# The order of the last weight loads in a decode kernel, and the queue that loads x

## The chip, the core and the metric

The kernel runs on one NeuronCore of a Trainium2 chip. The metric is the device time of one execution in microseconds (us), as the median of several runs. All inputs lie in HBM (the chip's main memory) as bfloat16, and the kernel moves them into SBUF (on-chip memory of 128 partitions) with DMA transfers that run on 16 DMA engines.

## The reference

One token per batch entry goes through an attention block with a sliding window over a key and value cache, and then through a gated MLP block. Batch B = 8, model width D = 512, 32 query heads, 8 key/value heads, head size 128, window W = 2048 of 8192 cached positions.

```python
def _A_ref(x, k_cache, v_cache, wq, wo):
    q = (x @ wq).reshape(B, 1, 32, 128).transpose(0, 2, 1, 3)
    k = repeat(k_cache[:, :, Sk - W:, :], 4, axis=1)
    v = repeat(v_cache[:, :, Sk - W:, :], 4, axis=1)
    p = softmax(einsum("bhqd,bhkd->bhqk", q, k) * 128 ** -0.5)
    o = einsum("bhqk,bhkd->bhqd", p, v)
    return o.transpose(0, 2, 1, 3).reshape(B, 1, 4096) @ wo

def _B_ref(x, w1, w2, w3, w4):
    # with one token every shifted branch is zero, so hs = 0 and x1 = x
    return x + gelu(layernorm(x) @ w3) @ w4

h   = x + _A_ref(layernorm(x), k_cache, v_cache, wq, wo)
out = h + _B_ref(layernorm(h), w1, w2, w3, w4)
```

The loads are: wq 4 MB, the windows of K and of V 32 MB each, wo 4 MB, w3 and w4 1.8 MB each. w1 and w2 are not needed, since the shifted branches vanish for one token.

## The kernel before, in words

The kernel is written engine by engine. Each engine (TensorE, ScalarE, VectorE, GpSimd, SyncE) gets its own list of instructions in a fixed order, and they meet only at semaphores. SyncE (SP) issues nearly all loads, in the order of the list `order`.

**Tiles and slots.** The K window of one batch entry and four heads is one tile of 2 MB, and so is the V window, so there are 16 K tiles (k0 to k15) and 16 V tiles (v0 to v15), two of each for a batch entry. A tile takes one of NS = 10 slots of the buffer `slots`, 16 KB in each of the 128 partitions. The n-th entry of `order` goes into slot n % 10. `free_slot(n)` makes SP wait until entry n - 10 is used up: for a K tile until TensorE has transposed it (`sem_Thi`), for a V tile until its product with the probabilities is done (`sem_PV`). The last two slots hold wq at first, and are free once the queries lie in `qstrip`.

**Order before.** SP first loads wq. Then come k0, k1, and for each batch entry two K tiles and two V tiles by turns. The end of the list is k15, v13, the first half of wo, v14, v15, the rest of wo, w3, w4. The last V tile v15 is loaded in two halves with semaphores of their own (`V_CUT`), wo in four pieces of 16, 8, 4 and 4 heads (`WO_CUT`), and w4 in two pieces of 8 and 6 chunks (`W4_CUT`). Behind v15 SP loads x a second time, into `xr_sb`. The first load of x, into `x_sb`, is issued by ScalarE in `act_warm`.

**The end of the kernel.** `act_exp`, `dve_pT` and `pe_PV` handle the last batch entry (b = 7) once its scores are complete. `pe_PV` multiplies each V tile in 64 matmuls. `dve_combine` writes the attention output into `oT_all`. `pe_proj` then adds x (4 matmuls with an identity) and the output projection, 4 matmuls for each of 32 heads, and waits before heads 0, 16, 24 and 28 for the piece of wo that it needs. `dve_h`, `pe_stats`, `dve_norms` and `act_std_h` form the layer norm of the sum. `pe_h3` waits for w3 and runs 56 matmuls, `act_gelu` follows, and `pe_fin` runs 28 matmuls over the 14 chunks of w4, with a wait at each entry of `W4_CUT`. The result is copied by VectorE and ScalarE and stored by SP.

**Start.** x is needed by `dve_pro1` (its layer norm) and by `pe_zinit`. wq is needed by `pe_q`, whose result VectorE writes into `qstrip`. The first eight K and V tiles need neither, since their slots are free from the start.

## Time and profile before

| What | Value |
|---|---|
| median of 4 runs | 198.11 us (197.84 to 198.3) |
| the profiled execution's own time | 198.49 us |
| its span, first to last instruction | 196.7 us |
| granted TensorE clock, mean | 0.894 |
| busy: TensorE matmul / weight load | 159.8 us / 119.4 us |
| busy: VectorE / ScalarE / GpSimd | 82.6 us / 90.5 us / 4.8 us |
| DMA queue 1 (all of SP's loads) | 10544 packets, 79.19 MB, 96.4% of 16 engines' span |
| DMA queue 8, kind "instruction" | 22 packets, 0.36 MB |

The profile is of one execution. It lies 0.38 us above the median of the four runs, and its own time is 1.8 us longer than its span, which begins with the first and ends with the last of the program's instructions. L409 means line 409 of the kernel file. PE is TensorE's matmul, PEld its weight load, DVE is VectorE, ACT is ScalarE, SPq is a DMA issue by SyncE. "Idle before" is the time that the engine stood idle before an instruction, with what ended it; "issue" there means that no semaphore that the profile shows ended it.

### The profile page before, as it was taken

Reading aid. Unit: us, or ns where it says so; the run is one execution under the profiler, and the core shown is the slowest. Engines: PE = TensorE matmul, PEld = TensorE weight load, DVE = VectorE, ACT = ScalarE, POOL = GpSimd, SP = SyncE. Lnnn points to the kernel's source line nnn. Section 1 sums busy time; section 2 is a strip of 40 time slices with the busy share of each in tenths; the row PEclk is TensorE's granted clock in tenths of the full one; section 3 lists DMA queues with packets and bytes.
Section 4 is the critical chain, followed back from the end, with each engine's and each line's share of the span. In section 5 each row is a group of like instructions: output and inputs, shape, how many; then the busy total and the mean of one; then the engine's idle time right before and its main releaser. Section 6 shows DMA issues by size and latency. Waiting matters only on the chain.

```text
span 196.7 us, 6328 instructions
## 1 busy us (share of the span) xinstructions
PE 159.8 (81%) x2808; PEld 119.4 (61%) x2808; DVE 82.6 (42%) x184; ACT 90.5 (46%) x109; POOL 4.8 (2%) x15
## 2 busy tenths in 40 slices
PE   2037999699989998959997989698989989385465
PEld 0037866486767766647775666576767767185452
DVE  7501445444662375425623653256236614330040
ACT  3301665936573465625643665247436534330040
POOL 8000000000000000000000000000000000000000
PEclk9999999999996999996999999969996969955555
DMA  6999999999999999999999999999999999999980
GB/s 228 433 420 427 443 423 430 430 427 427 428 427 430 432 423 433 423 430 427 430 427 430 427 433 430 422 437 423 433 427 423 427 390 390 425 402 314 407 337 14
DMA packets 10585, 79.58 MB, mean 405 GB/s; under 512 B 680, under 2 KB 4800, under 8 KB 6208
## 3 DMA queue, kind: packets, MB, share of 16 engines
q1 hardware_dynamic: 10544, 79.19, 96.4%
q8 instruction: 22, 0.36, 0.7%
q14 instruction: 3, 0.02, 0.0%
q10 hardware_dynamic: 16, 0.01, 0.0%
HBM read 79.18 MB, written 0.01 MB: 403 GB/s over the span
## 4 chain that ended last, share of the span: by engine, by line
DMA 56%; PE 28%; SPq 9%; issue 3%; DVE 2%; ACT 2%; ACTq 0%
DMA slots<-in_A_k_cache_dram 51%; PE kT_ps L409 16%; PE S_ps L441 6%; DMA slots<-in_A_wo_dram 5%; SPq L268 5%; SPq L262 3%; PE misc L533 3%; PE b L697 2%; DVE pT_sb L507 1%; ACT kT_sb L420 1%; PE misc L667 1%; ACT P_sb L475 1%; SPq L259 1%; PE S_ps L607 0%; PE S_ps L625 0%
## 5 line engine op out<-in xcount | busy, mean ns | idle before, releaser
L420 ACT ACTIVATE kT_sb<-kT_ps 128x1024 bf16<-128x1024 bf16 x64 | 65.6, 1025 | 75.4 <-PE kT_ps L409 75.4
L409 PEld LDWEIGHTS kT_ps<-ident_b,slots 128*128 128x128 bf16 x1024 | 65.1, 106 | 29.8 <-issue 21.4
L409 PE MATMUL kT_ps<-ident_b,slots 128*128 128x128 bf16 x1024 | 74.6, 234 | 7.7 <-DMA slots<-in_A_k_cache_dram 7.7
L426 DVE COPY kT_sb<-kT_ps 128x1024 bf16<-128x1024 bf16 x64 | 43.6, 688 | 61.9 <-PE kT_ps L409 61.9
L441 PE MATMUL S_ps<-kT_sb,qstrip 128*32 128x512 bf16 x256 | 38.4, 613 | 0.0
L533 PEld LDWEIGHTS misc<-pT_sb,slots 128*128 128x128 bf16 x1024 | 27.2, 97 | 7.8 <-issue 6.0
L533 PE MATMUL misc<-pT_sb,slots 128*128 128x16 bf16 x1024 | 28.6, 170 | 3.8 <-DVE pT_sb L507 1.9
L475 ACT ACTIVATE P_sb<-S_ps,mtile 128x1024 bf16<-128x1024 f32 x16 | 17.8, 1115 | 4.7 <-DVE mtile L464 4.4
L409 PE MATMUL kT_ps<-ident_b,P_sb 128*128 128x128 bf16 x128 | 10.0, 226 | 6.6 <-ACT P_sb L475 5.5
L409 PEld LDWEIGHTS kT_ps<-ident_b,P_sb 128*128 128x128 bf16 x128 | 7.5, 100 | 11.7 <-issue 4.9
L507 DVE TENSOR_TENSOR pT_sb<-kT_ps,maskT 128x1024 bf16<-128x1024 bf16 x16 | 10.4, 684 | 0.2
L441 PEld LDWEIGHTS S_ps<-kT_sb,qstrip 128*32 128x32 bf16 x256 | 5.9, 94 | 6.0 <-issue 0.6
L540 DVE TENSOR_TENSOR oT_all<-misc,rL 128x32 bf16<-128x32 f32 x8 | 2.4, 300 | 16.1 <-PE misc L533 16.1
L588 ACT ACTIVATE std<-var,eps_t 128x8 f32<-128x8 f32 x1 | 0.3, 301 | 14.4 <-DVE var L640 14.4
L453 DVE TENSOR_REDUCE mtile<-S_ps 128x1 f32<-128x512 f32 x8 | 5.5, 692 | 3.0 <-PE S_ps L441 3.0
L364 PE MATMUL S_ps<-xlnT,slots 128*128 128x8 bf16 x128 | 3.6, 168 | 3.2 <-DMA slots<-in_A_wq_dram 3.2
L607 PE MATMUL S_ps<-oT_all,slots 128*128 128x8 bf16 x128 | 3.9, 168 | 2.2 <-issue 1.6
L364 PEld LDWEIGHTS S_ps<-xlnT,slots 128*128 128x128 bf16 x128 | 3.5, 104 | 3.3 <-issue 3.3
L344 PE MATMUL b<-ident_b,xln_b 8*128 8x8 bf16 x4 | 0.3, 174 | 6.2 <-DVE xln_b L321 6.2
L607 PEld LDWEIGHTS S_ps<-oT_all,slots 128*128 128x128 bf16 x128 | 3.7, 104 | 2.3 <-issue 1.7
L297 DVE TENSOR_SCALAR ident_f<-iota_f 128x128 f32<-128x128 f32 x1 | 3.9, 3928 | 1.5 <-POOL iota_f L202 1.5
L344 PEld LDWEIGHTS b<-ident_b,xln_b 8*128 8x128 bf16 x4 | 0.2, 114 | 7.1 <-DVE xln_b L321 7.1
(75 smaller groups left out, 57.5 us busy)
## 6 DMA issues: line engine op xcount, KB each, us to landing
slots<-in_A_k_cache_dram SPq DMA_DIRECT2D x16, 2048.0 KB, 41.7
slots<-in_A_v_cache_dram SPq DMA_DIRECT2D x15, 2048.0 KB, 44.3
slots<-in_A_wq_dram SPq DMA_DIRECT2D x1, 4096.0 KB, 12.3
slots<-in_A_wo_dram SPq DMA_DIRECT2D x1, 2048.0 KB, 44.4
slots<-in_A_v_cache_dram SPq DMA_DIRECT2D x2, 1024.0 KB, 13.7
slots<-in_B_w_dram SPq DMA_DIRECT2D x1, 1792.0 KB, 12.0
slots<-in_A_wo_dram SPq DMA_DIRECT2D x1, 1024.0 KB, 16.2
slots<-in_A_wo_dram SPq DMA_DIRECT2D x2, 512.0 KB, 13.4
```

What stands on the lines that cost most here:

```text
L262: e.dma_start(dst, src).then_inc(sem_slot[slot], 16)
L268: e.dma_start(dst[:, f0:f0 + (h1 - h0) * D].rearrange("p (h n) -> p h n", n=D), A_wo[h0 * 128:h1 * 128, :].rearrange("(h p) n -> p h n", p ...
L364: ins = e.matmul(S_ps[:, 0, h * B:(h + 1) * B], wq_v[:, kc, h * DH:(h + 1) * DH], xlnT[:, kc * B:(kc + 1) * B], start=(kc == 0), stop=(kc ...
L409: ins = e.matmul(kT_ps[n % 2][:, c * 128:(c + 1) * 128], src[:, c * 128:(c + 1) * 128], ident_b[:, :], is_transpose=True)
L420: e.activation(kT_sb[:, i % NKT, 0:W // 2], kT_ps[step_of[("k", i)] % 2][:, 0:W // 2], ACT.Copy).then_inc(sem_Elo, 1)
L426: e.tensor_copy(kT_sb[:, i % NKT, W // 2:W], kT_ps[step_of[("k", i)] % 2][:, W // 2:W]).then_inc(sem_Ehi, 1)
L441: ins = e.matmul(S_ps[32 * gl:32 * (gl + 1), b % 2, :], qstrip[:, b, GL * gq + gl, o:o + 32], kv[:, gl, :, :], start=(gq == 0 and qi == 0) ...
L453: ins = e.tensor_reduce(mtile[:, 2, 0:1], S_ps[:, j, :], AX.X, ALU.max)
L475: e.activation(P_sb[:, half * W // 2:(half + 1) * W // 2].rearrange("r (k g) -> r k g", g=GL), s_rep, ACT.Exp, bias=mtile[:, j, 0:1], scal ...
L507: e.tensor_tensor(pT_sb[:, half * hc:(half + 1) * hc, :], kT_ps[n % 2][:, half * W // 2:(half + 1) * W // 2].rearrange("p (c x) -> p c x", ...
L533: ins = e.matmul(ot, slots[:, slot, c * DH:(c + 1) * DH], pt[:, cc, :, o:o + R], start=(n == 0), stop=(n == C - 1), skip_group_check=True)
L607: ins = e.matmul(hT_ps[:, k * B:(k + 1) * B], wo_at(h)[:, k * 128:(k + 1) * 128], oT_all[:, h, :], start=False, stop=(h == H - 1), skip_gr ...
```

## The change

x becomes the first load on SP, ahead of wq, and ScalarE issues no load any more. The second load of x is dropped: `pe_proj` reads `x_sb`, and has no wait for x. At the end of `order` the first half of wo moves behind v14 and v15, so that all of wo follows the last V tile, and w3 and w4 follow as before. w4 is cut into three pieces of 8, 4 and 2 chunks in place of two of 8 and 6. By the slot rule v14 now waits for k11, v15 for v9 and the first half of wo for k12, where before the first half of wo waited for k11, v14 for v9 and v15 for k12. What stands behind them waits for the same entries as before. No compute instruction is added or removed, and their order on each engine is unchanged.

```diff
-        xr_sb = sb([B, D], dt.bfloat16, "xr_sb")
...
-        sem_w4 = [S(f"sem_w4_{i}") for i in range(2)]
+        sem_w4 = [S(f"sem_w4_{i}") for i in range(3)]
...
-        W4_CUT = [0, 8, 14]
+        W4_CUT = [0, 8, 12, 14]
...
-        order += [("wo", 0), ("v", NTILE - 2), ("v", NTILE - 1), ("wo", 1), ("w3", 0), ("w4", 0)]
+        order += [("v", NTILE - 2), ("v", NTILE - 1), ("wo", 0), ("wo", 1), ("w3", 0), ("w4", 0)]
...
         def sp_prog(e):
+            e.dma_start(x_sb[:], A_x.rearrange("b s d -> (b s) d")).then_inc(sem_x, 16)
             e.dma_start(wq_sb, A_wq.rearrange("(p k) n -> p (k n)", k=KC)).then_inc(sem_wq, 16)
...
-                        e.dma_start(xr_sb[:], A_x.rearrange("b s d -> (b s) d")).then_inc(sem_xr, 16)
...
         def act_warm(e):
-            e.dma_start(x_sb[:], A_x.rearrange("b s d -> (b s) d")).then_inc(sem_x, 16)
             e.wait_ge(sem_pool, POOL_EPS)
...
         def pe_proj(e):
...
-            e.wait_ge(sem_xr, 16)
             for k in range(KC):
-                e.matmul(hT_ps[:, k * B:(k + 1) * B], xr_sb[:, k * 128:(k + 1) * 128], ident_b[0:B, 0:B],
+                e.matmul(hT_ps[:, k * B:(k + 1) * B], x_sb[:, k * 128:(k + 1) * 128], ident_b[0:B, 0:B],
                          start=(k == 0), stop=False, skip_group_check=True)
```

## The prediction

> **What bounds the kernel now.** I read the page's slices first.

> ```profile
> PEclk9999999999996999996999999969996969955555
> DMA  6999999999999999999999999999999999999980
> ```

> The DMA engines are full from the second of 40 slices to the 38th. TensorE is busy too (81%), but its waits at the start of a K tile end with that tile's load (7.7 us in 6 waits by the waits view), so the stream of loads sets the pace, and whatever delays its start delays the kernel. The clock stays at half speed in the last five slices.

> The start, from the timeline:

> ```profile
> 0.73 0.40 SPq L236 DMA_DIRECT2D slots<-in_A_wq_dram  x1
> 0.74 0.59 ACTq L287 DMA_DIRECT2D x_sb<-in_A_x_dram  x1
> 1.19 1.91 SPq L262 DMA_DIRECT2D slots<-in_A_k_cache_dram  x3
> ```

> The two issues run side by side. The first wq packet starts at 1.76, and by half-microsecond windows the engines are full from 2.5 on.

> SP's own timeline near the end:

> ```profile
> 124.04 0.38 SPq L268 DMA_DIRECT2D slots<-in_A_wo_dram  x1
> 126.28 36.59 SPq L262 DMA_DIRECT2D slots<-in_A_v_cache_dram  x1
> 162.92 1.33 SPq L259 DMA_DIRECT2D slots<-in_A_v_cache_dram  x2
> 164.30 0.54 SPq L260 DMA_DIRECT2D xr_sb<-in_A_x_dram  x1
> 164.88 11.54 SPq L268 DMA_DIRECT2D slots<-in_A_wo_dram  x3
> 176.46 2.02 SPq L272 DMA_DIRECT2D slots<-in_B_w_dram  x1
> 178.52 2.55 SPq L278 DMA_DIRECT2D slots<-in_B_w_dram  x2
> ```

> An issue behind a large wo piece is held: v14's for 36.59 us, the second wo piece of the later half for 9.04 of the 11.54. Loads still land in order, by their semaphores' updates: k15 158.2, v13 163.1, wo's first half 168.4, v14 173.3, v15's halves 175.8 and 178.3, the wo pieces 181.0, 182.5 and 184.1, w3 188.4, w4's pieces 191.0 and 192.9.

> The end, TensorE's timeline:

> ```profile
> 173.79 3.04 PE L533 MATMUL misc<-pT_sb,slots 128*128 128x16 bf16 x96
> 178.33 0.97 PE L533 MATMUL misc<-pT_sb,slots 128*128 128x16 bf16 x30 [1.49 <-DMA slots<-in_A_v_cache_dram]
> 179.63 0.22 PE L533 MATMUL misc<-pT_sb,slots 128*128 128x16 bf16 x2 [0.33 <-issue]
> ...
> 184.13 0.40 PE L607 MATMUL S_ps<-oT_all,slots 128*128 128x8 bf16 x9 [0.52 <-DMA slots<-in_A_wo_dram]
> 186.18 0.33 PE L607 MATMUL S_ps<-oT_all,slots 128*128 128x8 bf16 x7 [1.64 <-issue]
> ...
> 189.31 1.63 PE L667 MATMUL misc<-uT,slots 128*128 128x8 bf16 x56 [1.61 <-DVE uT L644]
> ...
> 191.30 3.16 PE L697 MATMUL b<-slots,gT 128*8 128x256 bf16 x28
> ```

> Two idle times bear the name "issue": 0.33 before the last two V matmuls and 1.64 inside the last wo piece, though that piece landed at 184.1. Exactly 127 matmuls, with their weight loads about 255 instructions, lie between the two places. Queue 8 carries 22 instruction packets of 16 KB; two of them run from 177.32 to 178.29 and from 183.97 to 184.93. So TensorE runs out of instructions, and goes on 1.2 us after such a packet ends. [...]

> **x ahead of wq on SP.** The nearest row for the price is the same 8 KB load on the same queue, L260: 0.54 us, and 0.04 between issues. The ACT row says 0.59. That puts wq at 1.31 in place of 0.73 and shifts the whole stream by up to 0.65. The lower bound: the first wq packet came 1.03 after its issue, the store's first packet at the end 0.80 after its own (194.96 to 195.76). If that 0.23 is a cost of first use that x now pays, 0.34 remains. Below nothing I exclude, as the wq issue cannot come sooner. I take 0.50. No slack absorbs it, since the engines are full from 2.5 to 178. x itself is hidden: its layer norm waits for VectorE's masks until 6.46. The nine K and V issues behind wq end by 6.4 and become 0.5 later, with wq's packets covering them until 12. ScalarE loses 0.59 of issue time that nothing waits for.

> **The second load of x goes.** 8 packets of some 0.05 us on eight engines, 0.54 us of SP time under full queues, a wait that was long met: -0.05 at most.

> **The order at the end.** The bytes ahead of each wo piece but the first, of w3 and of w4 are the same, so those landings only move by the start's shift. v14 and v15 land one wo half earlier (168.0, then 170.5 and 173.0), and wo's first half at 178.3 in their place, each plus 0.5. Their slots are free in time: k11 and v9 released SP at 124.04 and 126.28, and k12's transposes end at 134.4, forty microseconds ahead of the data. SP's hold behind wo's first half comes later, until about 172.6 (when, as at 162.88 before, about half of its 2048 rows have been moved), and w3's issue becomes some 1 us later than the 176.46 to 178.48 of before. Only w3, w4 and the store stand behind on SP; w3 is needed by the slowest engine at 184.1. Price nothing, under that cover of 4 us; without it, the last rival.

> On TensorE the 1.49 us wait for v15 goes: k15 and the softmax chain still release the V matmuls at 173.79 + 0.5, and 128 at 31.7 ns (3.04 us for 96) would end at 177.85 + 0.5. What is late next is the instruction block, at 179.63 + 0.5 if its packet is as slow as before, then the next at 186.18 + 0.5. So the layer norm, L667 and the start of L697 follow 0.5 later. [...]

> [...]

> **w4 in three pieces.** One more issue, 1.2 us of SP (L278) while its queue is full, and one more wait on TensorE that holds the last four matmuls and the output copy behind it. L697's 28 matmuls ran without a gap before (28 x 105 ns from 191.30), so a smaller last piece has nothing to win unless L697 starts sooner: 0.

> **Sum.** 0.50 - 0.05 - 0 - 0 = +0.45. On the profiled execution that is 198.49 + 0.45 = 198.94, which lies 0.38 above its median; on the median 198.11 + 0.45 = 198.56, say 198.55. A measurement here tells 0.2%, 0.4 us, from no change.

> **Rivals.** [...]

> *Clock regained: faster.* Without the 1.49 us hole TensorE works from 172.6 to 178.3 nearly without a break. The clock's records show it coming back after whole stretches of 3.41 us of K work (158.48 to 161.89). At full clock L697 shrinks from 2.95 to some 1.8 (16 transposes take 1.00 against 1.69), and the end is w4's last piece, 192.9 + 0.5, plus four matmuls and the drain: 193.95 against 194.48, so 197.6. It decides only if V matmuls of 16 columns count as work and the clock then survives the waits for wo. Against: a stretch with 1.7 us of them and a 0.65 gap lost the clock at 158.48, and 5 us of end work did not bring it back.

> [...]

> *Starved by wo.* 4 MB in 1 KB rows now stand in one piece. If wo's next issue is held as long behind the first half as it was before (9.04 us), it comes free at 181.6, while the slowest engine is through at 178.3: with 1 us to the first packet 4.3 us are lost, 202.4, and a hold of half the excess 200.5. It decides once the hold ends after 178. Against: the hold before ended when V's rows ahead were drained, and none stand between now.

> **How the numbers follow.** Forecast +0.35 to +0.65: 0.55. Looser tail: 0.20. Clock regained: 0.14. Starved: 0.11. Slower by over 0.2% is most of the forecast (those over 0.4 us) and the starved case, 0.47 + 0.11 = 0.58; within is the looser tail and the forecast's low end, 0.28; faster 0.14. The range 197.5 to 199.6 takes in the first three and the mild starved cases.

> **What would show it.** Right: L235 (wq) issued near 1.3, k0 landing near 18.4 for 17.9, the last landing near 193.4, no DMA wait at v15's matmuls but "issue" there, and again inside the last wo piece. Wrong: wq's first packet near 1.8 all the same; a granted clock over 0.5 after 175; a wait for wo beyond 178.8; landings of w3 that move by more than the start's shift.

## The result, and the profile after

The changed kernel is slightly slower. Its median is 198.93 us over 54 runs, against 198.36 us over 78 runs of the kernel before, and the ratio is 1.0027 with a 95% interval of 1.0018 to 1.0036. That is +0.53 us on 198.36, where the sum of the prediction gave +0.45 on its own base. The profiled executions of two experiments below (e1 and e4) were slow ones, with spans of 235.2 and 287.9 us, so only their first microseconds are read, and their times come from the other runs.

The start, from the timeline of the kernel after:

```profile
0.73 1.28 ACT L286 ACT_TABLE_LOAD   x1 [0.73 <-PEq L744]
0.73 0.37 SPq L234 DMA_DIRECT2D x_sb<-in_A_x_dram  x1
1.16 0.37 SPq L235 DMA_DIRECT2D slots<-in_A_wq_dram  x1
```

The issue of x took 0.37 us on SP, and with 0.06 to the next issue wq comes 0.43 us later than before (1.16 against 0.73). By the semaphores' updates wq lands at 13.49 for 13.05, k0 at 18.30 for 17.89, and k15 at 158.80 for 158.17.

SP's timeline at the end:

```profile
118.76 7.41 SPq L260 DMA_DIRECT2D slots<-in_A_v_cache_dram  x2
127.88 5.88 SPq L258 DMA_DIRECT2D slots<-in_A_v_cache_dram  x2
133.85 43.75 SPq L266 DMA_DIRECT2D slots<-in_A_wo_dram  x4
177.64 1.28 SPq L270 DMA_DIRECT2D slots<-in_B_w_dram  x1
```

v14 and v15 are issued by 133.8, and the hold moves behind the first half of wo. The issue of the second piece of wo, from 138.28 on, is held until 173.53, and w3 is issued 1.2 us later than before. The four wo pieces land at 178.8, 181.5, 182.9 and 184.2, w3 at 188.6, and the pieces of w4 at 191.1, 192.5 and 193.1.

TensorE's timeline at the end:

```profile
174.12 3.53 PE L530 MATMUL misc<-pT_sb,slots 128*128 128x16 bf16 x126
180.09 0.22 PE L530 MATMUL misc<-pT_sb,slots 128*128 128x16 bf16 x2 [2.44 <-issue]
...
186.68 0.33 PE L603 MATMUL S_ps<-oT_all,slots 128*128 128x8 bf16 x7 [1.99 <-issue]
187.52 0.69 PE L621 MATMUL S_ps<-hcat,mean_w 128*128 128x64 f32 x2 [0.51 <-DVE hcat L614]
189.81 1.64 PE L663 MATMUL misc<-uT,slots 128*128 128x8 bf16 x56 [1.61 <-DVE uT L640]
...
191.80 2.69 PE L693 MATMUL b<-slots,gT 128*8 128x256 bf16 x28
```

The wait for v15 is gone, but the time it took now stands before the last two V matmuls as 2.44 us named "issue". From there every step comes 0.46 to 0.50 us later than before: 180.09 for 179.63, 186.68 for 186.18, 189.81 for 189.31, 191.80 for 191.30. Only the last 28 matmuls are shorter in this one execution, 2.69 for 3.16 us. The windows of the kernel after say why (the columns are the stretch, its length, busy time of each engine, then the granted clock, the DMA share and the rate):

```profile
192.00:193.80 1.80, 1.80 (x20) 1.20 (x18) 0.00 (x0) 0.00 (x0) 0.00 (x0) 0.50 0.09 35
193.80:194.50 0.70, 0.69 (x12) 0.29 (x8) 0.00 (x0) 0.00 (x0) 0.00 (x0) 0.95 0.00 0
```

The granted clock is 0.50 from 169.97 to 193.87 and 1.00 from there on, for the last 12 matmuls. So the two profiled spans are equal, 196.7 us each, although the medians differ: one execution in which the clock came back hides the 0.5 us that the rest of the chain shows. That the two executions lie so evenly 0.5 us apart is in part chance, since executions differ by more than that: in e2, e3 and e9 below, where wq starts as early as before, the last 28 matmuls start at 190.52, 191.30 and 191.70. The loss rests on the medians and on the runs below.

### The profile page after: what moved, and what is told of

Same layout as the page of the kernel before. It is cut to its first block, busy times and chain, and to the rows that moved or that the text cites. A ratio compares the mean times of both kernels' runs of the same rounds, so it can differ in the third digit from the quotient of the medians.

```text
span 196.7 us, 6328 instructions
## 1 busy us (share of the span) xinstructions
PE 159.5 (81%) x2808; PEld 119.3 (61%) x2808; DVE 82.4 (42%) x184; ACT 90.8 (46%) x109; POOL 4.8 (2%) x15
## 2 busy tenths in 40 slices
DMA  6999999999999999999999999999999999999980
## 4 chain that ended last, share of the span: by engine, by line
DMA 56%; PE 29%; SPq 5%; issue 4%; DVE 3%; ACT 3%; ACTq 0%; DVEq 0%
DMA slots<-in_A_k_cache_dram 52%; PE kT_ps L406 16%; PE S_ps L438 7%; SPq L266 4%; DMA slots<-in_A_wo_dram 4%; PE misc L530 3%; ACT P_sb L472 1%; PE b L693 1%; ACT kT_sb L417 1%; PE misc L663 1%; DVE pT_sb L504 1%; PE S_ps L603 0%; DVE mtile L450 0%; PE S_ps L621 0%; PE b L684 0%
## 5 line engine op out<-in xcount | busy, mean ns | idle before, releaser
L406 PE MATMUL kT_ps<-ident_b,P_sb 128*128 128x128 bf16 x128 | 10.6, 231 | 6.8 <-ACT P_sb L472 5.7
L481 DVE TENSOR_TENSOR lsum<-lcol 128x1 f32<-128x1 f32 x8 | 1.3, 158 | 8.3 <-ACT P_sb L472 8.3
```

Source lines behind the costliest of these rows:

```text
L406: ins = e.matmul(kT_ps[n % 2][:, c * 128:(c + 1) * 128], src[:, c * 128:(c + 1) * 128], ident_b[:, :], is_transpose=True)
```

## The experiments

The theory is that the later start of wq sets the whole loss and the order at the end is neutral, since the end would be held by TensorE's instruction packets and by landings that the order does not move. The rivals are that the order costs, that the order helps and the start hides it, and that the idle times named "issue" have another cause. All ratios are to the kernel before on the same chip.

**e1: the start alone.** To the kernel before:

```diff
         def sp_prog(e):
+            e.dma_start(x_sb[:], A_x...).then_inc(sem_x, 16)
             e.dma_start(wq_sb, A_wq...).then_inc(sem_wq, 16)
...
         def act_warm(e):
-            e.dma_start(x_sb[:], A_x...).then_inc(sem_x, 16)
```

> The kernel before with one edit: x is the first load on SP ahead of wq, and ScalarE loads nothing. Theory (the late start of wq sets the loss): wq is issued near 1.16 instead of 0.73, k0 lands near 18.3 instead of 17.9, the last load lands 0.43 us later, and the time is +0.43 us or ratio 1.002 against before. Rival (the order at the end sets the loss): the time is that of before within 0.1 us, ratio 1.000, although k0 lands later.

Measured: ratio 1.0034, interval 1.0016 to 1.0052 (median 198.76 for 198.17). SP's timeline of e1:

```profile
1.17 0.36 SPq L237 DMA_DIRECT2D slots<-in_A_wq_dram  x1
```

This edit alone gives a loss that cannot be told from that of the full change, and the rival's 1.000 is outside. k0 lands at 18.50, for 18.3 expected. The later landings come from the other traces. In the seven with wq first (before, e2, e3, e5, e7, e8, e9) k15 lands between 157.99 and 158.27, in the two with x first (after, e6) at 158.80 and 158.65. The last piece of w4 lands at 192.36 to 192.94 in the seven, 192.6 on the mean, and at 193.11 and 192.92 in the two. So some 0.4 us of the late start are still there when the loads end.

**e2: the order alone.** To the kernel after:

```diff
         def sp_prog(e):
-            e.dma_start(x_sb[:], A_x...).then_inc(sem_x, 16)
             e.dma_start(wq_sb, A_wq...).then_inc(sem_wq, 16)
...
         def act_warm(e):
+            e.dma_start(x_sb[:], A_x...).then_inc(sem_x, 16)
```

> The kernel after with one edit undone: wq is first on SP again and x comes from ScalarE's queue; all of wo stays behind the last V tiles, w4 in three pieces, no second load of x. Theory: no difference to before beyond 0.1 us, ratio 1.000; no DMA wait at v15's matmuls, about 2 us of idle time named issue before the last two V matmuls and again within the last wo piece. Rival (the order at the end costs): +0.4 us, ratio 1.002. Second rival (the order helps and the start hides it): -0.3 us or more, ratio 0.9985 or less.

Measured: ratio 0.9994, interval 0.9976 to 1.0011 (median 198.03 for 198.17). A cost of 1.002 is excluded. A gain of 0.0015, the second rival, is not: 0.9985 lies within the interval, so by the times the order costs at most 0.2 us and gains at most 0.5. TensorE's timeline of this run has both idle times:

```profile
178.46 0.22 PE L530 MATMUL misc<-pT_sb,slots 128*128 128x16 bf16 x2 [2.57 <-issue]
...
185.33 0.33 PE L603 MATMUL S_ps<-oT_all,slots 128*128 128x8 bf16 x7 [1.39 <-issue]
```

**e3: x on SP, but second.** To the kernel after, the first two loads of SP exchanged:

```diff
-            e.dma_start(x_sb[:], A_x...).then_inc(sem_x, 16)
             e.dma_start(wq_sb, A_wq...).then_inc(sem_wq, 16)
+            e.dma_start(x_sb[:], A_x...).then_inc(sem_x, 16)
```

> The kernel after with the first two loads on SP exchanged: wq first, x second, both on SP. Theory (only the place of wq in the queue counts, not which engine loads x): wq is issued at 0.73 and k0 lands near 17.9, the time is that of before within 0.1 us, ratio 1.000; x lands behind wq's first packets, still before VectorE needs it at 6.46. Rival (x in SP's queue costs wherever it stands): ratio 1.002. If x lands after 6.5 us, its layer norm comes later, but wq lands only at 13, so that costs nothing until about 9 us.

Measured: ratio 1.0012, interval 0.9996 to 1.0029, which excludes neither theory. k0 lands at 17.75, as expected. x did not land behind the first packets of wq but behind all of it. The timeline of e3:

```profile
1.18 0.36 SPq L235 DMA_DIRECT2D x_sb<-in_A_x_dram  x1
...
13.05 0.68 DVE L312 BATCH_NORM_STATS2 st<-x_sb 8x6 f32<-8x512 bf16 x1 [6.52 <-DMA x_sb<-in_A_x_dram]
```

The layer norm is 6.6 us late, so the first K transposes start at 20.28 for 17.93. K15 still lands at 158.20, and the last 28 matmuls start at 191.30, both as before. In this execution a delay of 2.35 us on TensorE at the start was made up, since the loads went on meanwhile; the interval of the times, up to 1.0029, does not show that it cost nothing. The loads' own start, 0.44 us later in e1, was not made up. ScalarE loads nothing in e3 either, as in e1, and yet wq lands as early as before (12.90 for 13.05), so it was the place ahead of wq that made the stream late, and not the engine that loads x.

**e4: the suspected cost twice.** To the kernel after, x loaded a second time ahead of wq, into a buffer that the projection reads:

```diff
             e.dma_start(x_sb[:], A_x...).then_inc(sem_x, 16)
+            e.dma_start(xr_sb[:], A_x...).then_inc(sem_xr, 16)
             e.dma_start(wq_sb, A_wq...).then_inc(sem_wq, 16)
```

> The kernel after with a second 8 KB load ahead of wq on SP (x again, into a buffer of its own that the projection reads): the suspected cost is doubled. Theory: wq is issued near 1.59, k0 lands near 18.75, the time is +0.86 us against before, ratio 1.0043, that is +0.43 us against after. Rival (a cost of first use that is paid once): +0.43 us against before, as after.

Measured: ratio 1.0051, interval 1.0033 to 1.0069 (median 199.14 for 198.17). SP's timeline:

```profile
0.73 0.37 SPq L236 DMA_DIRECT2D x_sb<-in_A_x_dram  x1
1.17 0.27 SPq L237 DMA_DIRECT2D xr_sb<-in_A_x_dram  x1
1.49 0.37 SPq L238 DMA_DIRECT2D slots<-in_A_wq_dram  x1
```

wq is 0.76 us late, less than the 0.86 expected as the second issue takes 0.27, and the ratio gives about 1.0 us. A cost paid once was put at 1.002, which lies outside the interval. But e1 measured 1.0034 for one issue, and that lies just inside it, so the times point to a loss that grows with the number of issues and do not show it. Nor do the landings of this one execution: the first packet of wq starts at 2.49, 0.34 us later than in the kernel after, yet k0 lands at 18.38 for 18.75 expected, and for 18.30 there.

**e5 and e6: the place in TensorE's stream.** To the kernel before (e5) and after (e6), 64 tiny matmuls while TensorE has nothing to do at the start:

```diff
         def pe_zinit(e):
...
+            for _ in range(64):
+                e.matmul(S_ps[:, 0, 0:B], zrow_b[0:1, :], x_sb[0:1, 0:B], start=True, stop=True)
```

> The kernel before with 64 tiny matmuls (zeros added over zeros, 8 columns) in TensorE's idle time at the start, behind its first two: nothing of the end is edited, but every instruction of the end stands 128 places (half a 16 KB packet) later in TensorE's stream. Theory (TensorE waits for instruction packets): the idle times named issue leave the last two V matmuls and the last wo piece; one remains in the middle of the projection; the projection ends near 184.6 instead of 186.5, and the last 28 matmuls start at w4's first landing, 191.03 instead of 191.30. Time -0.27 us, ratio 0.9986. Rival (the idle times come from something else, such as the semaphores of wo): they stay at the same matmuls, ratio 1.000.

> The kernel after with the same 64 tiny matmuls at the start. Theory: the late start (+0.43 us) and the freed end (last 28 matmuls from w4's first landing, about 191.4, instead of 191.8) nearly cancel: ratio to before 1.000 to 1.001, that is 0.002 below after. Rival (the packets do not bind): 1.0027 as after.

Measured: e5 0.9988, interval 0.9975 to 1.0001; e6 1.0009, interval 0.9996 to 1.0023. Both lie where the theory put them. In e6 the rival's 1.0027 is excluded; in e5 its 1.000 is not, and there the trace decides. The two ran on the same chip and are 0.39 us apart (medians 198.09 and 198.48): the full change costs about as much in kernels whose end stands 128 instructions later in TensorE's stream. TensorE's timeline of e5:

```profile
178.28 1.02 PE L535 MATMUL misc<-pT_sb,slots 128*128 128x16 bf16 x32 [1.45 <-DMA slots<-in_A_v_cache_dram]
...
183.74 0.59 PE L609 MATMUL S_ps<-oT_all,slots 128*128 128x8 bf16 x16 [0.67 <-DMA slots<-in_A_wo_dram]
184.84 0.69 PE L627 MATMUL S_ps<-hcat,mean_w 128*128 128x64 f32 x2 [0.51 <-DVE hcat L620]
188.12 1.66 PE L669 MATMUL misc<-uT,slots 128*128 128x8 bf16 x56 [2.58 <-DMA slots<-in_B_w_dram]
```

No "issue" is left at either place, although nothing of the end was edited. The matmuls of the last wo piece run through as soon as it lands, the norm begins 2.2 us sooner (184.84 for 187.02), and TensorE now waits 2.58 us for w3, which lands at 188.07. In e6 one idle time of 0.33 us named "issue" appears 57 matmuls into the projection, which is 64 matmuls ahead of its old place (121 into the projection):

```profile
178.63 1.68 PE L605 MATMUL S_ps<-oT_all,slots 128*128 128x8 bf16 x57 [0.76 <-DMA slots<-in_A_wo_dram]
180.64 0.33 PE L605 MATMUL S_ps<-oT_all,slots 128*128 128x8 bf16 x7 [0.33 <-issue]
```

**e7, e8 and e9: a version that is faster than both.** e7 is e2 with the 64 tiny matmuls and

```diff
-        W4_CUT = [0, 8, 12, 14]
+        W4_CUT = [0, 2, 4, 6, 8, 10, 12, 14]
```

with seven semaphores. e8 has the same two edits on the kernel before, so it keeps the old order. e9 is e7 without the tiny matmuls.

> wq first on SP and x from ScalarE's queue as before, all of wo behind the last V tiles as after, the 64 tiny matmuls at the start, and w4 in seven pieces of two chunks. Theory: the norm is done by about 187.5, w3 lands at 188.4, the last 28 matmuls start near 190.5 and follow the pieces, and end about 0.6 us after the last landing at 192.9, near 193.5 instead of 194.48: time -0.9 to -1.0 us, ratio 0.995. Rival (the small pieces or SP's issues cost what they win): ratio 0.9985 or more, as with the shift alone.

> The kernel before (half of wo ahead of the last two V tiles, second load of x) with the 64 tiny matmuls and w4 in seven pieces: what e7 has, without the order of after. Theory (the order is neutral, since wo's last piece, w3 and w4 land at the same time in both): ratio 0.995 as e7, within 0.001. Rival (the order pays once the end is freed, since the V matmuls need not wait for v15): 0.001 or more above e7.

> e7 without the 64 tiny matmuls: wq first on SP, x from ScalarE, all of wo behind the last V tiles, w4 in seven pieces. Theory (small pieces win nothing while instruction packets hold the start of the last 28 matmuls past w4's first landing): about 2 us of idle time named issue in the last wo piece again, the last 28 matmuls start near 191.2, ratio 0.999 to 1.000. Rival (the small pieces alone made e7 fast): ratio 0.995 to 0.996.

Measured: e7 0.9951, interval 0.9934 to 0.9969 (median 197.29 for 198.30). e8 0.9956, interval 0.9940 to 0.9971 (197.49). e9 0.9999, interval 0.9977 to 1.0022. TensorE's timeline of e7:

```profile
183.69 0.59 PE L605 MATMUL S_ps<-oT_all,slots 128*128 128x8 bf16 x16 [0.77 <-DMA slots<-in_A_wo_dram]
184.79 0.69 PE L623 MATMUL S_ps<-hcat,mean_w 128*128 128x64 f32 x2 [0.51 <-DVE hcat L616]
188.11 1.66 PE L665 MATMUL misc<-uT,slots 128*128 128x8 bf16 x56 [2.63 <-DMA slots<-in_B_w_dram]
...
190.12 3.16 PE L695 MATMUL b<-slots,gT 128*8 128x256 bf16 x28
```

and of e9:

```profile
186.58 0.33 PE L603 MATMUL S_ps<-oT_all,slots 128*128 128x8 bf16 x7 [2.33 <-issue]
...
191.70 3.16 PE L693 MATMUL b<-slots,gT 128*8 128x256 bf16 x28
```

The last 28 matmuls take 3.16 us in both, but start at 190.12 with the shift and at 191.70 without it. Not all of that is the shift, as the profiled execution of e9 took 198.96 us, 1.0 above the median of its runs (197.93). What decides is the ratio of e9: the 0.995 to 0.996 that the small pieces alone would have to give lie outside its interval. Fine pieces of w4 paid only where the idle times named "issue" no longer held the start, and the shift alone paid little (e5, 0.9988), as the first large piece of w4 held it then (a wait of 0.46 us). The two together give 1.0 us. e7 and e8 differ by 0.0005, far inside their intervals. So the order at the end is worth little in the faster kernel too; the 0.001 of the rival is not excluded.

## Why the prediction was right, step by step

**x ahead of wq.** The step held: e1 shows the loss with this edit alone, and the landings show some 0.4 us of the shift still there at the end. The value taken, 0.50, was close to the 0.43 by which wq's issue moved and the 0.39 by which its first packet did. The row it leaned on was a little too dear: L260 took 0.54 late in the kernel, with the DMA engines full, while the same load took 0.37 at the start, with the DMA engines idle (a DMA share of 0.00 in the windows up to 1.50 before). The first packet of wq came at 2.15 (1.76 before), 0.99 us after its issue, where it was 1.03 before, and not 0.80, so x took over only some 0.04 us of that.

**The second load of x.** No run leaves it out alone. e1 keeps it and loses as much as the full change, so the 0.05 credited for dropping it is neither shown nor excluded.

**The order at the end.** v14, v15 and the first three pieces of wo land within 0.1 us of the prediction, which added 0.50 to the landings of before. The last piece of wo, w3 and w4 land 0.3 to 0.4 us sooner than that (193.11 for the last one, where 193.4 was named); among the seven executions above the last landing spreads over 0.6 us. The new hold of SP behind wo ended at 173.53 for the 172.6 + 0.5 predicted, w3 was issued 1.2 us later for "some 1 us", and nothing waited for it. That settles the starved rival: its turning point was 178. (Its prices do not quite follow from its terms: they leave out the 0.50 of the start, and half of its 4.3 us gives 200.3, not 200.5.) e2 agrees with a price of nothing, within the 0.2 us of cost and 0.5 us of gain that its interval leaves.

**What is late next.** The V matmuls lost their wait for v15, and the idle time named "issue" took its place, as predicted: 180.09 for the predicted 180.13, 186.68 for 186.68. That the two numbers match so closely is luck, as the same places lie at 178.46 and 185.33 in e2 and at 179.98 and 186.58 in e9, both with the early start. e5 and e6 show that these idle times are not waits on data, since they move with the position in TensorE's stream. That TensorE waits there for an instruction packet is argued from the rows: in the kernel before the two idle times end 1.34 and 1.25 us after the end of a packet (178.29 and 184.93), in the kernel after 1.58 and 1.25 us (178.51 and 185.43). The 0 that the sum takes here was an estimate, and no run shows a rule for when a packet comes. What the traces show is that from the first matmul behind each idle time to the start of the next packet it was 4.3 and 4.6 us (179.63 to 183.97, 186.18 to 190.74), and 4.4 and 4.6 in the kernel after, and that the last 28 matmuls start 0.50 later (191.80 for 191.30). A looser tail, in which TensorE comes past the second place sooner and the last 28 matmuls start at w4's first landing (191.03 before), did not come: from one idle time named "issue" to the next it is 6.59 us, for 6.55 before. One reading of the prediction was off without harm to the sum: the V matmuls took 28 ns each (3.53 us for 126), not 31.7, since the row of 96 contains a short wait for the first half of v15, which landed at 175.77.

**w4 in three pieces.** Nothing to be seen of it in e2, as predicted; e9 finds the same for seven, and e7 shows what is needed for it to pay.

**Clock regained.** It did not come by the V matmuls: 3.53 us of them from 174.12, directly behind the transposes, left the clock at 0.50, and the rival's hole-free stretch was there. The clock did come back at 193.87 in the profiled execution, which the prediction would have counted as a sign against itself (a clock over 0.5 after 175). It came behind a stretch of steady matmuls from 189.81 on, and shortened the last 28 by 0.47 us in that execution. In the profiled execution of e3 these 28 took 2.78 us, in those of e2, e5 to e9 and of the kernel before 3.15 to 3.27. What decides it was not tried. In the traces of before and after the changes of the clock lie whole multiples of 3.41 us apart (3.41 to 37.55). Of the kernel after, the stretch from 173.38 to 176.80 has TensorE busy throughout (3.42 of 3.42 us), nearly all of it V matmuls of 16 columns, and the clock stayed at 0.50; the one from 190.45 to 193.87 is as full, most of it matmuls of 128 and 256 columns, and the clock behind it was 1.00. So a full stretch alone was not enough here, and what else it took is not shown.

## What to carry to other kernels

Here one stream of loads kept the DMA engines full from the second of 40 slices to the 38th, and a 0.4 us issue in front of its first large load cost 0.4 to 0.7 us, while 2.35 us lost on TensorE at the start (e3) cost less than 0.6 us and perhaps nothing. Before loads are reordered, see what releases the last step: here the idle time named "issue" moved with the place in the instruction stream, and the order of loads could not touch it. Smaller last pieces paid here only together with an edit that let the work on them start as soon as the first had landed (e7 and e8, not e9).

## What the runs showed of the hardware that was not expected

In e3 the 8 KB load of x, behind the 4 MB of wq on the same queue, waited for nearly all of it: it was issued at 1.18, its packets ran from 12.07 to 12.51, and VectorE could start on it at 13.05, with wq landing at 12.90, while from ScalarE's queue in the kernel before its packets started at 1.70 beside those of wq.
